# First-stage sums as 208 rows in two overlapping blocks, with the first groups of the second stage loaded and the last chunks stored in another order

## The chip, the cores and the metric

The kernel runs on one core of a Trainium2 chip. The metric is the device time of one launch in microseconds: the median of three runs before the change is 2804.82 us (2800.7 to 2805.57).

## The reference

A long convolution, then two feed-forward layers, all in float32. Cut to what is computed:

```python
h_filt = (np.maximum(pos_emb @ w1, 0.0) @ w2) * np.exp(-0.01 * pos)[:, None]   # (12480, 128)
u = x * v                                                                      # (2, 12480, 128)
y = irfft(rfft(u, 2 * S, axis=1) * rfft(h_filt, 2 * S, axis=0), 2 * S)[:, :S]  # S = 12480
z = (x * y).reshape(24960, 128)
g = np.maximum(z @ moe_w_in, 0.0) ** 2          # d_ff = 2048
z = g @ moe_w_out
h = z @ moe2_w_in
out = (h * np.cos(h)) @ moe2_w_out
```

## The kernel before

The position index of 12480 is split into 104 x 120, and the transform is done in stages of matrix products on TensorE.

**Stage 1** (to about 245 us) runs over 30 chunks `q` of two columns `i`, 60 pairs in all. SyncE (SP) loads a chunk in one transfer `ld` of 128 x 2720 floats, 1360 KB: x, v, the twiddle table and the positions. Five slots hold chunks; SP issues the load of chunk q+5 when TensorE is done with chunk q. `mlp1` and `prep` make the filter and the product x*v up to five pairs ahead. `pair` (L190) multiplies by the twiddles: for each of two halves `a` of the positions it does one product for the real and one for the imaginary parts `r`, each with 112 output rows (104 and 8 of padding) and 384 columns; ScalarE (ACT) copies one half out as `v` (L200) and VectorE (DVE) writes sum and difference into `bt` (L202). `store` (L205) sends `bt`, 112 rows of 3072 floats, to the DRAM tensor `Bs` from ACT's queue, one pair after the chunk is done. Three `bt` buffers go round. In between, SP loads 16 pieces `wr` of the later layers' weights, and `decode` splits them.

**Stage 2** (about 256 to 494 us) runs over 26 groups of four rows. `load2` (L134) brings a group from `Bs` into `B2`: up to 128 partitions of four pieces of 768 floats. `spectrum` (tile `H`) transforms the filter part, `product` (`Z`) the signal part, `hi` and `hr` (L291 to L302) are copies of `H`, and `inverse`, `inv_copy` (tile `ds`, L358) and `half` (tile `dt`) finish a group, which `keep` stores to `Ds`. Three `B2` slots go round, in the memory that chunks held before.

**Stage 3** (to the end, 2803.7 us) does the last transform (`pc`) and the two layers; TensorE is its bound.

Each engine takes its instructions in the order written here. A transfer that is issued from SP or ACT counts as one: if it has to wait, what stands behind it on that engine waits too. The built program gives the transfers eight completion counters in turn, so an issue can also wait for the last user of its counter. Between stages 1 and 2 the kernel before does the following. While chunks 26, 27 and 28 run, SP loads 96 of the 128 partitions of groups 0, 1 and 2. Group 0's rest comes from `Bs` (16 rows, after the first 16 rows of chunk 27 are stored) and by `direct` (L212): eight transfers of one row each from `bt` of chunks 28 and 29 to `B2[0]`. ACT stores chunks 27, 28 and 29 in two parts, 16 rows first and 96 later. Tiles of stage 2 take the memory of stage 1's tiles, `hi` that of `bt`.

Of the kernel before, what the change touches and what calls it, by code (L numbers as in the profile page):

```python
# [23 lines left out]
NP = 112  # L24
# [15 lines left out]
R = 96  # L40
FIRST = 384 + 4 * NCH + 4 * NP
XVE, SLOT = 2048 + 4 * NP, 3072
# [12 lines left out]
def conv_moe(ctx, tc, t):  # L55
    nc = tc.nc
    cst = ctx.enter_context(tc.tile_pool(name="cst", bufs=1))
    Bs, Ds = t["Bs"], t["Ds"]
# [71 lines left out]
    def load2(g, a=0, b=128):  # L130

        if g not in B2:
            B2[g] = slot("B2").rearrange("p (k c e) -> p k c e", k=G4, c=2)
        nc.sync.dma_start(out=B2[g][a:b].rearrange("p k c e -> p k (c e)"),  # L134
                          in_=bass.AP(Bs.tensor, G4 * g * 4 * HB * 384 + 768 * a,
                                      [[768, b - a], [4 * HB * 384, G4], [1, 768]]))


    with ExitStack() as st:
        c1 = st.enter_context(tc.tile_pool(name="c1", bufs=1))  # L140
# [8 lines left out]
        win = first[0:NP, 384:384 + 4 * NCH].rearrange("p (q i a) -> p q i a", q=NCH, i=CB)  # L149
        emid = first[0:NP, 384 + 4 * NCH:FIRST].rearrange("p (a r k) -> p a r k", a=2, r=2)  # L150
        ld = {}

        def load(q):
            sl = slot("ld", *((ring, SLOT) if q % LDB < NB else (ring1, XVE + CB * NP)))
            nc.sync.dma_start(out=sl[:, 0:XVE + CB * NP], in_=t["ld"][q])
            x, v = (sl[0:NP, 1024 * n:1024 * (n + 1)].rearrange("p (i a d) -> p i a d", i=CB, a=2) for n in range(2))
            et = sl[0:NP, 2048:XVE].rearrange("p (a r k) -> p a r k", a=2, r=2)
            pt = sl[:, XVE:XVE + CB * NP].rearrange("p (i k) -> p i k", i=CB)
            ld[q] = (pt, x, v, et)

        def turned(q, i, a, r):

            if i == 0:
                return ld[q][3][:, a, r, :]
            return ld[q][3][:, 1 - a, 1 - r, :] if q else emid[:, a, r, :]
# [62 lines left out]
        for n, (q, i) in enumerate(seq):  # L228
# [5 lines left out]
            if i == 0 and 0 < q < NCH - 2:  # L234
                store(q - 1)
# [534 lines left out]
```

## Time and profile before

| what | value |
|---|---|
| median of three runs | 2804.82 us (2800.7 to 2805.57) |
| profiled execution, its own time | 2805.52 us |
| its span, first to last instruction | 2803.7 us |
| TensorE busy | 2742.0 us, 98% of the span |
| DVE, ACT, POOL busy | 85%, 86%, 49% |
| mean share of the DMA engines | eight tenths or more in each of the first seven of 40 slices, three and less later |
| HBM read and written | 140.29 MB and 79.63 MB |

A whole-span share says little here, since the three stages have different limits: after 500 us TensorE is busy almost without a gap, and before it is not. The DMA engines are full in the first 250 us and then nearly idle from 500 us on. So the profile is to be read by stages, the first 260 us above all. Rates in the rows are GB/s over all 16 DMA engines of the core. A busy share of a DMA engine counts a transfer from its start, also while it waits for memory, so a share near 1 can go with different rates.

### The profile page before, as it was taken

To read this page: it belongs to the slowest core of one execution; us is meant where nothing else is said; L and a number is where in the kernel's file an instruction comes from. 1 tells how busy PE (TensorE), PEld (TensorE's weight loads), DVE (VectorE), ACT (ScalarE), POOL (GpSimd) and SP (SyncE) were. 2 spreads that over 40 slices of the span, in tenths; PEclk is the share of its full clock that TensorE was granted. 3 is DMA by queue.
4 is the path that set the end of the run, shared out by engine and by line. 5 is a ranking of instruction groups with operands and counts; after the bars stand their busy time and mean duration, and the time that the engine had idled before them with its cause. 6 is when DMAs were issued, how large, how long until landed. Compare 5 with 4: busy or idle time off the path is not lost.

```text
span 2803.7 us, 38672 instructions
## 1 busy us (share of the span) xinstructions
PE 2742.0 (98%) x11740; PEld 2109.9 (75%) x11740; DVE 2380.7 (85%) x4673; ACT 2410.7 (86%) x4294; POOL 1362.3 (49%) x1050
## 2 busy tenths in 40 slices
PE   8897999999999999999999999999999999999999
PEld 4453444788888888888888888888888888888887
DVE  5775999788888888888888888888888888888888
ACT  4444999799999999999999999999999999999998
POOL 4554888144444444444444444444444444444445
PEclk9998999999999999999999999999999999999999
DMA  9998898310111110101010101011001011101000
GB/s 371 385 378 271 291 298 255 87 30 16 31 28 31 28 32 16 33 27 31 28 31 16 34 25 31 28 32 28 25 22 31 28 32 28 31 17 32 16 9 10
DMA packets 83287, 222.54 MB, mean 79 GB/s; under 512 B 5582, under 2 KB 49190, under 8 KB 75878
## 3 DMA queue, kind: packets, MB, share of 16 engines
q1 hardware_dynamic: 78719, 177.99, 19.8%
q10 hardware_dynamic: 4359, 42.08, 3.8%
q8 instruction: 93, 1.52, 0.2%
q14 instruction: 116, 0.95, 0.1%
HBM read 140.29 MB, written 79.63 MB: 78 GB/s over the span
## 4 chain that ended last, share of the span: by engine, by line
PE 86%; ACT 7%; DMA 4%; issue 2%; DVE 1%; POOL 0%; ACTq 0%; SPq 0%; DVEq 0%; POOLq 0%
PE h L525 13%; PE h L527 13%; PE y L541 13%; PE y L540 13%; PE h L526 13%; PE y L539 13%; PE pc L491 4%; PE A L198 4%; DMA ld<-ld 3%; ACT w L320 2%; ACT w L321 1%; ACT hi L291 1%; ACT hr L300 1%; PE hp L184 1%; ACT ds L358 1%
## 5 line engine op out<-in xcount | busy, mean ns | idle before, releaser
L630 POOL TENSOR_TENSOR gl<-g,gh 128x512 fp32r<-128x512 f32 (+2 forms) x800 | 1042.7, 1303 | 1268.2 <-ACT gh L621 747.7
L613 DVE TENSOR_TENSOR g<-h,c 128x512 f32<-128x512 f32 (+2 forms) x800 | 539.2, 674 | 246.4 <-ACT c L605 240.6
L590 ACT ACTIVATE k<-h,quarter 128x512 int32<-128x512 f32 (+2 forms) x800 | 541.2, 677 | 135.5 <-PE h L527 133.2
L525 PE MATMUL h<-zh,wh 128*128 128x512 f32 (+2 forms) x1600 | 634.1, 396 | 1.1 <-DVE zh L509 0.8
L541 PE MATMUL y<-gl,wh 128*128 128x512 f32 (+2 forms) x1600 | 624.1, 390 | 3.9 <-POOL gl L630 2.2
L527 PE MATMUL h<-zh,wl 128*128 128x512 f32 (+2 forms) x1600 | 625.0, 391 | 0.0
L540 PE MATMUL y<-gh,wh 128*128 128x512 f32 (+2 forms) x1600 | 624.2, 390 | 0.0
L539 PE MATMUL y<-gh,wl 128*128 128x512 f32 (+2 forms) x1600 | 622.4, 389 | 0.1
L526 PE MATMUL h<-zl,wh 128*128 128x512 f32 (+2 forms) x1600 | 621.8, 389 | 0.0
L605 ACT ACTIVATE c<-r,halfpi 128x512 f32<-128x512 f32 (+2 forms) x800 | 565.6, 707 | 2.6 <-DVE r L598 2.6
L564 ACT ACTIVATE r<-h 128x512 f32<-128x512 f32 (+2 forms) x800 | 472.2, 590 | 78.9 <-PE h L527 78.8
L584 DVE TENSOR_TENSOR gl<-g,gh 128x512 fp32r<-128x512 f32 (+2 forms) x800 | 536.8, 671 | 1.1
L598 DVE CUSTOM_DVE_ANT_0 r<-h,k 128x512 f32<-128x512 f32 (+2 forms) x800 | 536.6, 671 | 0.0
L570 ACT ACTIVATE g<-r 128x512 f32<-128x512 f32 (+2 forms) x800 | 493.1, 616 | 1.0 <-DVE gl L584 0.4
L577 DVE CAST gh<-g 128x512 fp32r<-128x512 f32 (+2 forms) x800 | 332.2, 415 | 45.0 <-ACT g L570 40.5
L541 PEld LDWEIGHTS y<-gl,wh 128*128 128x128 f32 x1600 | 301.4, 188 | 75.1 <-POOL gl L630 7.5
L527 PEld LDWEIGHTS h<-zh,wl 128*128 128x128 f32 x1600 | 301.8, 189 | 68.3
L540 PEld LDWEIGHTS y<-gh,wh 128*128 128x128 f32 x1600 | 301.6, 188 | 68.4
L539 PEld LDWEIGHTS y<-gh,wl 128*128 128x128 f32 x1600 | 301.6, 188 | 66.6 <-DVE zl L552 0.9
L525 PEld LDWEIGHTS h<-zh,wh 128*128 128x128 f32 x1600 | 302.1, 189 | 65.8 <-issue 1.0
L526 PEld LDWEIGHTS h<-zl,wh 128*128 128x128 f32 x1600 | 301.8, 189 | 60.4
L621 ACT ACTIVATE gh<-g 128x512 fp32r<-128x512 f32 (+2 forms) x400 | 246.4, 616 | 0.1
(63 smaller groups left out, 2415.9 us busy)
## 6 DMA issues: line engine op xcount, KB each, us to landing
ld<-ld SPq DMA_DIRECT2D x30, 1360.0 KB
Bs<-bt ACTq DMA_DIRECT2D x27, 1344.0 KB
B<-Bs SPq DMA_DIRECT2D x23, 1536.0 KB
dt<-Ds SPq DMA_DIRECT2D x59, 416.0 KB
Ds<-dt SPq DMA_DIRECT2D x24, 960.0 KB
xt<-xT SPq DMA_DIRECT2D x60, 208.0 KB
out<-o SPq DMA_DIRECT2D x47, 256.0 KB
tt<-T SPq DMA_DIRECT2D x60, 169.0 KB
```

What stands on the lines that cost most here:

```text
L525: nc.tensor.matmul(h[:, :n], wh[:, f, :], zh[:, :n], start=True, stop=False)
L526: nc.tensor.matmul(h[:, :n], wh[:, f, :], zl[:, :n], start=False, stop=False)
L527: nc.tensor.matmul(h[:, :n], wl[:, f, :], zh[:, :n], start=False, stop=True)
L539: nc.tensor.matmul(y[:, :n], wl[:, f, :], gh[:, :n], start=a, stop=False)
L540: nc.tensor.matmul(y[:, :n], wh[:, f, :], gh[:, :n], start=False, stop=False)
L541: nc.tensor.matmul(y[:, :n], wh[:, f, :], gl[:, :n], start=False, stop=b)
L584: nc.vector.tensor_tensor(out=gl[:, :n], in0=g[:, :n], in1=gh[:, :n].bitcast(F32), op=ALU.subtract)
L590: nc.scalar.activation(k[:, :n], hp[2, u][:, :n], AF.Identity, scale=-1.0, bias=quarter)
L598: nc.vector._custom_dve(TENSOR_ADD_SAT, out=r[:, :n], in0=h[:, :n], in1=k[:, :n], s0=0.25, s1=-0.75)
L605: nc.scalar.activation(c[:, :n], r[:, :n], AF.Sin, bias=halfpi, scale=TWO_PI)
L613: nc.vector.tensor_tensor(out=g[:, :n], in0=h[:, :n], in1=c[:, :n], op=ALU.mult)
L630: nc.gpsimd.tensor_tensor(out=gl[:, :n], in0=g[:, :n], in1=gh[:, :n].bitcast(F32), op=ALU.subtract)
```

## The change

Stage 1's twiddle table keeps real and imaginary rows interleaved without padding: 208 rows. `pair` computes them as two blocks of 128 rows, 0 to 127 and 80 to 207, so that 48 rows are computed twice; the number of products, of columns and of copies per pair stays as it is, on 128 partitions where there were 112. A chunk's load has 2672 floats a row instead of 2720 (1336 KB). A chunk's store is two transfers, 128 and 80 rows of 1536 floats (768 and 480 KB) instead of one of 112 rows of 3072 (1344 KB).

Between the stages: groups 0 and 1 are loaded in full, 128 partitions, after chunk 27 is stored. Rows of chunks 28 and 29 that groups 0 to 3 need (32 rows of `Bs`) go to a small tensor `Bx` by `store_late`, and from there into `B2` by `load_late`, over what the full load put there; a transfer at the start of the kernel fills that part of `Bs` with other data, so that it holds something. `direct` is down to four rows, all of chunk 29. The last pair runs in two halves of one block each, with the last two direct rows and `store_late` issued between them. The remaining stores of chunks 28 and 29 go out on SP, behind the load of group 2. `bt` gets memory of its own (`out1`), and in stage 2 that memory is taken by `ds` and `dt` (pool `lk`), which are first written later than `hi`. In stage 3 the pools of layer 2 come first, so that they lie where `ds` and `dt` were.

On SP this is the end of stage 1, from the second-last `wr` to the loads of groups 3 and 4, before (`B2_1400`, `B2_1441`, `B2_1477` are groups 0, 1, 2; `bt_1466`, `bt_1498` are chunks 28 and 29):

```order
L84 DMA wr_1280<-moe2_w_in 128x1024
L155 DMA ld_1325<-ld 128x2720
L84 DMA wr_1371<-moe2_w_out 128x4x256
L134 DMA B2_1400<-Bs 96x4x768
L134 DMA B2_1441<-Bs 96x4x768
L134 DMA B2_1477<-Bs 96x4x768
L134 DMA B2_1400<-Bs 16x4x768
L212 DMA B2_1400<-bt_1466 1x4x768 x2
L212 DMA B2_1400<-bt_1498 1x4x768 x2
L134 DMA B2_1441<-Bs 32x4x768
L134 DMA B2_1477<-Bs 32x4x768
L134 DMA B2_1630<-Bs 128x4x768
```

And now (`B2_1506`, `B2_1508`, `B2_1561` are groups 0, 1, 2; `bt_1493`, `bt_1526` are chunks 28 and 29):

```order
L86 DMA wr_1400<-moe2_w_out 128x4x256
L136 DMA B2_1506<-Bs 128x4x768
L136 DMA B2_1508<-Bs 128x4x768
L143 DMA B2_1506<-Bx 2x4x768 x2
L232 DMA B2_1506<-bt_1526 1x4x768 x3
L143 DMA B2_1508<-Bx 4x4x768 x2
L136 DMA B2_1561<-Bs 128x4x768
L218 DMA Bs<-bt_1493 96x1536
L218 DMA Bs<-bt_1493 80x1536
L218 DMA Bs<-bt_1526 96x1536
L218 DMA Bs<-bt_1526 80x1536
L143 DMA B2_1561<-Bx 4x4x768 x2
```

The loads of groups 0 and 1 stand whole behind the last `wr`, and four stores stand on SP behind group 2's load.

On ACT this is the stretch from the copy of pair (28, 0) to the first copy of stage 2, before (`bt_1429` is chunk 27):

```order
L200 ACTIVATE v_1473<-A_1467 112x768
L205 DMA Bs<-bt_1429 16x3072
L205 DMA Bs<-bt_1429 96x3072
L200 ACTIVATE v_1491<-A_1485 112x768
L109 ACTIVATE wh21_73<-w_a_1445 128x512
L200 ACTIVATE v_1505<-A_1499 112x768
L205 DMA Bs<-bt_1466 16x3072
L212 DMA B2_1400<-bt_1466 1x4x768 x2
L205 DMA Bs<-bt_1466 96x3072
L200 ACTIVATE v_1522<-A_1516 112x768
L212 DMA B2_1400<-bt_1498 1x4x768 x2
L205 DMA Bs<-bt_1498 16x3072
```

And now, up to the first `hi` (`bt_1457` is chunk 27):

```order
L211 ACTIVATE v_1496<-A_1494 128x768
L218 DMA Bs<-bt_1457 128x1536
L218 DMA Bs<-bt_1457 80x1536
L211 ACTIVATE v_1515<-A_1513 128x768
L111 ACTIVATE wh21_73<-w_a_1472 128x512
L211 ACTIVATE v_1529<-A_1527 128x768
L218 DMA Bx<-bt_1493 32x1536
L211 ACTIVATE v_1545<-A_1543 128x384
L232 DMA B2_1506<-bt_1526 1x4x768
L218 DMA Bx<-bt_1526 32x1536
L211 ACTIVATE v_1545<-A_1543 128x384
L319 ACTIVATE hi0_1599<-H_1597 64x512
```

ACT issues three transfers behind chunk 27's stores where it issued eight, and no store of 96 rows stands ahead of the last pair's copy or of `hi`.

The diff, without the tables on the host and what only follows the new shapes:

```diff
@@ -21,7 +21,8 @@
-NP = 112
+KR = 2 * N1
+SPLIT = KR - 128
@@ -37,9 +38,10 @@
-R = 96
-FIRST = 384 + 4 * NCH + 4 * NP
-XVE, SLOT = 2048 + 4 * NP, 3072
+LATE = NCH - 2
+KE = 32
+FIRST = 384 + 4 * NCH + 2 * KR
+XVE, SLOT = 2048 + 2 * KR, 3072
@@ -127,16 +129,23 @@
-    def load2(g, a=0, b=128):
-
-        if g not in B2:
-            B2[g] = slot("B2").rearrange("p (k c e) -> p k c e", k=G4, c=2)
-        nc.sync.dma_start(out=B2[g][a:b].rearrange("p k c e -> p k (c e)"),
-                          in_=bass.AP(Bs.tensor, G4 * g * 4 * HB * 384 + 768 * a,
-                                      [[768, b - a], [4 * HB * 384, G4], [1, 768]]))
+    def load2(g):
+
+        B2[g] = slot("B2").rearrange("p (k c e) -> p k c e", k=G4, c=2)
+        n = 128 if g < NG - 1 else 2 * HB
+        nc.sync.dma_start(out=B2[g][0:n].rearrange("p k c e -> p k (c e)"),
+                          in_=bass.AP(Bs.tensor, G4 * g * 2 * HB * 768, [[768, n], [2 * HB * 768, G4], [1, 768]]))
+
+    def load_late(g, n=CB * (NCH - LATE)):
+
+        for r in range(2):
+            a = HB * r + CB * LATE
+            nc.sync.dma_start(out=B2[g][a:a + n].rearrange("p k c e -> p k (c e)"),
+                              in_=Bx[2 * G4 * g + r:2 * G4 * (g + 1):2, 0:n].rearrange("k p e -> p k e"))
...
+        out1 = st.enter_context(tc.tile_pool(name="out1", bufs=BT))
...
-            sl = slot("ld", *((ring, SLOT) if q % LDB < NB else (ring1, XVE + CB * NP)))
-            nc.sync.dma_start(out=sl[:, 0:XVE + CB * NP], in_=t["ld"][q])
+            sl = slot("ld", *((ring, SLOT) if q % LDB < NB else (ring1, XVE + CB * N1)))
+            nc.sync.dma_start(out=sl[:, 0:XVE + CB * N1], in_=t["ld"][q])
...
-        def pair(q, i):
+        def pair(q, i, between=None):
             if i == 0:
-                bt_t[q] = io.tile([NP, CB, 2, 2, 384], F32, tag="bt", name="bt", bufs=BT)
+                bt_t[q] = out1.tile([128, 2, CB, 2, 384], F32, tag="bt", name="bt")
             u, bt = ut_t[q], bt_t[q]
-            A = {}
-            for a in (1, 0):
-                A[a] = psA.tile([NP, 2, 512], F32, tag="A", name="A")
-                for r in range(2):
-                    nc.tensor.matmul(A[a][:, r, 0:384], turned(q, i, a, r), u[:, i, a, :], start=True, stop=True)
-            v = wk.tile([NP, 2, 384], F32, tag="v", name="v")
-            nc.scalar.activation(v, A[1][:, :, 0:384], AF.Copy)
-            for c, op in ((0, ALU.add), (1, ALU.subtract)):
-                nc.vector.tensor_tensor(out=bt[:, i, :, c, :], in0=A[0][:, :, 0:384], in1=v, op=op)
-
-        def store(q, rows=slice(0, NP), eng=nc.scalar):
-            eng.dma_start(out=Bs[rows, 8 * q:8 * (q + 1), :].rearrange("k x e -> k (x e)"),
-                                in_=bt_t[q][rows].rearrange("k b r c e -> k (b r c e)"))
-
-        def direct(q):
-
-            for n in range(2 * CB):
-                eng = nc.scalar if n % 2 else nc.sync
-                eng.dma_start(out=B2[0][2 * CB * q + n:2 * CB * q + n + 1].rearrange("p k c e -> p (k c e)"),
-                              in_=bt_t[q][0:G4, n // 2, n % 2].rearrange("k c e -> k (c e)"))
+            A = {a: psA.tile([128, 2, 512], F32, tag="A", name="A") for a in (1, 0)}
+            v = wk.tile([128, 2, 384], F32, tag="v", name="v")
+            for ms in ((0,), (1,)) if between else ((0, 1),):
+                part = slice(ms[0], ms[-1] + 1)
+                for a in (1, 0):
+                    for m in ms:
+                        nc.tensor.matmul(A[a][:, m, 0:384], turned(q, i, a)[:, SPLIT * m:SPLIT * m + 128], u[:, i, a, :],
+                                         start=True, stop=True)
+                nc.scalar.activation(v[:, part], A[1][:, part, 0:384], AF.Copy)
+                for c, op in ((0, ALU.add), (1, ALU.subtract)):
+                    nc.vector.tensor_tensor(out=bt[:, part, i, c, :], in0=A[0][:, part, 0:384], in1=v[:, part], op=op)
+                if between and part.start == 0:
+                    between()
+
+        def put(eng, out, q, m, a, b):
+            eng.dma_start(out=out, in_=bt_t[q][a:b, m].rearrange("p i c e -> p (i c e)"))
+
+        def store(q, eng=nc.scalar):
+            a = KE if q >= LATE else 0
+            put(eng, Bs[a:128, CB * q:CB * (q + 1)].rearrange("p x e -> p (x e)"), q, 0, a, 128)
+            put(eng, Bs[128:KR, CB * q:CB * (q + 1)].rearrange("p x e -> p (x e)"), q, 1, 256 - KR, 128)
+
+        def store_late(q):
+            x = CB * (q - LATE)
+            put(nc.scalar, Bx[:, x:x + CB].rearrange("p x e -> p (x e)"), q, 0, 0, KE)
+
+        def direct(q, i, r, eng=nc.sync):
+
+            p = HB * r + CB * q + i
+            eng.dma_start(out=B2[0][p:p + 1].rearrange("p k c e -> p (k c e)"),
+                          in_=bt_t[q][r:2 * G4:2, 0, i].rearrange("k c e -> k (c e)"))
...
+        def last():
+            direct(NCH - 1, 1, 0)
+            direct(NCH - 1, 1, 1, nc.scalar)
+            store_late(NCH - 1)
+
         upto("load", load, LDB, NCH)
+        nc.sync.dma_start(out=Bs[0:KE, CB * LATE:HB].rearrange("p x e -> p (x e)"),
+                          in_=bass.AP(t["ld"].tensor, 0, [[CB * (NCH - LATE) * 768, KE], [1, CB * (NCH - LATE) * 768]]))
...
-            pair(q, i)
+            pair(q, i, last if n == len(seq) - 1 else None)
             upto("mlp", mlp1, (n + lead + 1) // CB + 1 if n else 1, NCH)
-            if i == 0 and 0 < q < NCH - 2:
-                store(q - 1)
-            if i == 0 and q >= NCH - 4 and q - NCH + 4 < NB:
-                load2(q - NCH + 4, 0, R)
-            if i == 0 and q >= NCH - 2:
-                store(q - 1, slice(0, 16))
-                if q == NCH - 2:
-                    load2(0, R, 2 * CB * q)
-                else:
-                    direct(q - 1)
-                store(q - 1, slice(16, NP))
+            if i == 0 and q:
+                if q > LATE:
+                    store_late(q - 1)
+                if q < NCH - 1:
+                    store(q - 1)
+            if (q, i) == (LATE, 0):
+                load2(0)
+                load2(1)
+            if (q, i) == (NCH - 1, 0):
+                load_late(0, CB * (NCH - 1 - LATE))
+                direct(q, 0, 0)
+                direct(q, 0, 1)
             if (q, i) == (NCH - 1, 1):
-                direct(q)
-                store(q, slice(0, 16))
-                for g in range(1, NB):
-                    load2(g, R)
-                store(q, slice(16, NP))
+                load_late(1)
+                load2(2)
+                store(q - 1, nc.sync)
+                store(q, nc.sync)
+                load_late(2)
...
-            s = wk.tile([2 * HB, 2, 256], F32, tag="ds", name="ds", bufs=4)
+            s = lk.tile([2 * HB, 2, 256], F32, tag="ds", name="ds", bufs=4)
...
-                dt_t[g] = hk.tile([2 * HB, 2, G4, 256], F32, tag="dt", name="dt")
+                dt_t[g] = lk.tile([2 * HB, 2, G4, 256], F32, tag="dt", name="dt")
...
                 load2(seq[n][0] + NB)
+                if 2 * G4 * (seq[n][0] + NB) < KE:
+                    load_late(seq[n][0] + NB)
...
-    t["Bs"] = nc.dram_tensor("Bs", (NP, 4 * HB, 384), F32).ap()
+    t["Bs"] = nc.dram_tensor("Bs", (KR, HB, 768), F32).ap()
+    t["Bx"] = nc.dram_tensor("Bx", (KE, CB * (NCH - LATE), 768), F32).ap()
```

## Rows read from the trace of the kernel before

**Rows 1.** Busy time of each engine by stretch, in us, with clock, DMA share, GB/s.
```profile
core 0: us, PE busy (x) PEld busy (x) DVE busy (x) ACT busy (x) POOL busy (x), PEclk, DMA share, GB/s
20.00:218.00 198.00, 174.80 (x558) 102.58 (x557) 148.65 (x198) 89.42 (x194) 104.32 (x75) 0.95 0.99 379
218.00:245.00 27.00, 27.00 (x82) 14.67 (x80) 20.51 (x30) 11.65 (x22) 13.79 (x11) 0.94 1.03 364
245.00:263.00 18.00, 6.35 (x9) 2.52 (x8) 1.82 (x2) 0.81 (x1) 0.99 (x1) 0.62 0.88 261
263.00:480.00 217.00, 213.67 (x493) 92.26 (x493) 204.61 (x320) 209.68 (x354) 185.30 (x149) 0.99 0.84 272
```
**Rows 2.** Chain of waits, 20 to 236 us: start, length, what.
```profile
by line: PE A L198 44.8%; DMA ld<-ld 41.3%; PE hp L184 8.1%; PE hp L172 4.9%; issue 0.7%; DVE bt L202 0.5%; SPq L155 0.1%; DVEq L202 0.0%
...
43.63 13.11 DMA ld<-ld
...
205.40 11.46 DMA ld<-ld
```
**Rows 3.** DMA queues, 60 to 200 us (q1 is SP's, q10 is ACT's).
```profile
q1 hardware_dynamic: 6520, 28.91, 56.1%
q10 hardware_dynamic: 2238, 24.16, 42.4%
```
**Rows 4.** DMA queues, 235 to 236 us: packets, MB, share.
```profile
q10 hardware_dynamic: 37, 0.38, 89.6%
q1 hardware_dynamic: 36, 0.10, 25.9%
```
**Rows 5.** Short stretches by engine, columns as in rows 1.
```profile
50.00:54.00 4.00, 3.02 (x11) 1.43 (x9) 3.88 (x4) 1.44 (x3) 4.00 (x4) 1.00 1.01 430
...
273.00:275.00 2.00, 1.88 (x5) 0.91 (x6) 1.85 (x4) 1.95 (x4) 2.00 (x3) 1.00 0.98 387
286.00:289.00 3.00, 3.00 (x8) 1.30 (x7) 2.80 (x6) 2.93 (x6) 2.88 (x3) 1.00 0.82 182
498.00:501.00 3.00, 2.22 (x12) 1.99 (x11) 1.81 (x8) 0.20 (x1) 0.00 (x0) 0.53 0.95 371
```
**Rows 6.** Groups of instructions by line and shape, 0 to 560 us.
```profile
L198 PE MATMUL A<-ut,ld 112*112 112x384 f32 x472 | 173.9, 515 | 0.8 <-ACT ut L186 0.8
L202 DVE TENSOR_TENSOR bt<-A,v 112x768 f32<-112x768 f32 x120 | 109.2, 952 | 76.1 <-PE A L198 64.7 <-ACT v L200 10.1 <-issue 0.5
```
**Rows 7.** ACT's instructions in order of time, 234 to 264 us.
```profile
236.65 1.86 ACTq L205 DMA_DIRECT2D Bs<-bt  x2
...
248.07 0.32 ACTq L205 DMA_DIRECT2D Bs<-bt  x1
248.49 0.81 ACT L200 ACTIVATE v<-A 112x768 f32<-112x768 f32 x1 [6.45 <-DMA Bs<-bt]
...
263.09 0.59 ACT L291 ACTIVATE hi<-H 64x512 f32<-64x512 f32 x1 [13.78 <-DMA B<-Bs]
```
**Rows 8.** TensorE's instructions in order of time, 230 to 285 us.
```profile
231.95 13.06 PE L198 MATMUL A<-ut,ld 112*112 112x384 f32 x40
256.66 3.75 PE L285 MATMUL H<-B,Gt 120*128 120x512 f32 x4 [11.65 <-DMA B<-bt]
...
265.54 1.61 PE L285 MATMUL H<-B,Gt 120*128 120x512 f32 x2 [2.24 <-ACT hr L300]
...
274.94 1.02 PE L285 MATMUL H<-B,Gt 120*128 120x512 f32 x2
```
**Rows 9.** Chain of waits, 236 to 270 us: start, length, what.
```profile
236.65 7.38 DMA Bs<-bt
...
244.12 8.24 DMA B<-Bs
...
254.28 8.55 DMA Bs<-bt
```
**Rows 10.** SP's transfers in order of issue, 200 to 300 us.
```profile
205.40 0.33 SPq L155 DMA_DIRECT2D ld<-ld  x1
...
222.32 22.10 SPq L134 DMA_DIRECT2D B<-Bs  x4
244.51 8.75 SPq L212 DMA_DIRECT2D B<-bt  x4
```
**Rows 11.** All engines in order of time, 275 to 278 us.
```profile
276.49 0.60 ACT L358 ACTIVATE ds<-d 120x512 f32<-120x512 f32 x1
```

More of the change, by code (lines that the diff above doesn't have):

```diff
@@ L148, in conv_moe, with turned @@
         w1b, w2b = first[:, 0:128], first[:, 128:384]
[L149 to L150 removed]
+        win = first[0:N1, 384:384 + 4 * NCH].rearrange("p (q i a) -> p q i a", q=NCH, i=CB)
+        emid = first[0:N1, 384 + 4 * NCH:FIRST].rearrange("p (a m) -> p a m", a=2)
         ld = {}
         def load(q):
[L154 to L158 removed]
+            sl = slot("ld", *((ring, SLOT) if q % LDB < NB else (ring1, XVE + CB * N1)))
+            nc.sync.dma_start(out=sl[:, 0:XVE + CB * N1], in_=t["ld"][q])
+            x, v = (sl[0:N1, 1024 * n:1024 * (n + 1)].rearrange("p (i a d) -> p i a d", i=CB, a=2) for n in range(2))
+            et = sl[0:N1, 2048:XVE].rearrange("p (a m) -> p a m", a=2)
+            pt = sl[:, XVE:XVE + CB * N1].rearrange("p (i k) -> p i k", i=CB)
             ld[q] = (pt, x, v, et)
[L161 removed]
+        def turned(q, i, a):
             if i == 0:
[L164 to L165 removed]
+                return ld[q][3][:, a]
+            return ld[q][3][:, 1 - a] if q else emid[:, a]
         ut_t, hT_t = {}, {}
@@ L215, in conv_moe @@
+        def direct(q, i, r, eng=nc.sync):
+            p = HB * r + CB * q + i
+            eng.dma_start(out=B2[0][p:p + 1].rearrange("p k c e -> p k (c e)"),
+                          in_=bt_t[q][r:2 * G4:2, 0, i].rearrange("k c e -> k (c e)"))
         nc.scalar.dma_start(out=first, in_=t["first"])
@@ L436, in conv_moe @@
     conv_st.close()
+    zk, ek, gk = {}, {}, {}
+    for layer in (2, 1):
+        zk[layer], ek[layer], gk[layer] = (ctx.enter_context(tc.tile_pool(name=f"{n}{layer}", bufs=2)) for n in ("zk", "ek", "gk"))
     ck = ctx.enter_context(tc.tile_pool(name="ck", bufs=2))
-    zk, ek, gk = {}, {}, {}
-    for layer in (1, 2):
-        zk[layer], ek[layer], gk[layer] = (ctx.enter_context(tc.tile_pool(name=f"{n}{layer}", bufs=2)) for n in ("zk", "ek", "gk"))
     psh = ctx.enter_context(tc.tile_pool(name="psh", bufs=1, space=PSUM))
@@ L694, in tables @@
         C, Z = np.cos(p), np.sin(p)
-        o = turns()
-        G[0::2, c, 0:60], G[1::2, c, 0:60] = C[o], Z[o]
-        G[0::2, c, 64:124], G[1::2, c, 64:124] = -Z[o], C[o]
+        for n, o in enumerate(turns()):
+            re, im = (HB + n, n) if n % CB and n > 1 else (n, HB + n)
+            G[re, c, 0:60], G[im, c, 0:60] = C[o], Z[o]
+            G[re, c, 64:124], G[im, c, 64:124] = -Z[o], C[o]
         I[0:60, c, 0::2], I[64:124, c, 0::2] = C.T, -Z.T
@@ L702, in tables @@
     first = np.zeros((128, FIRST))
-    first[0:NP, 384 + 4 * NCH:] = pad(pad(E[NCH], 0), 3).reshape(NP, 4 * NP)
+    first[0:N1, 384 + 4 * NCH:] = E[NCH]
     win = paired(win.reshape(N1, 2, HB), 0, 2).transpose(0, 2, 3, 1)
     first[0:N1, 384:384 + 4 * NCH] = win.reshape(N1, 4 * NCH)
-    return {"E": f(pad(pad(E[0:NCH], 1), 4)), "first": f(first), "G": f(G), "IG": f(I)}, T
+    return {"E": f(E[0:NCH]), "first": f(first), "G": f(G), "IG": f(I)}, T
 def turns():
```

27 lines of the change are left out of this document (11 added, 16 removed).

## Prediction

> **What bounds the kernel now.** I read the stretches first [rows 1]. After 480 us nothing of the change computes, and TensorE is the bound there. From 263 to 480 us ACT is busy 209.68 of 217 us and DVE 204.61: stage 2 runs at the pace of these two, and its start is what can be moved. That leaves two stretches. From 20 to 218 us TensorE has 174.80 us of work in 198, so 23.2 us of idle time, while the DMA engines are at a share of 0.99 and move 379 GB/s. From 245 to 263 us nearly everything stands: TensorE 6.35 us busy, ACT 0.81.
>
> The chain of waits says what TensorE waits for in the first stretch: 41.3% of 20 to 236 us, some 89 us, is the landing of a chunk's load, in seven round trips between 11.27 and 14.89 us, of which two stand in [rows 2]. A slot comes free, the load is issued, and it lands 13 us later, because it shares the engines with the stores: from 60 to 200 us SP's queue has 56.1% of the time and ACT's 42.4% [rows 3]. Where both queues have work they alternate one piece for one piece, 36 to 37 in one microsecond, although ACT's carried 0.38 MB and SP's 0.10 [rows 4].
>
> In the second stretch the chain has three landings one after another: a store 7.38 us, the last 16 rows of group 0 8.24 us, and the last store 8.55 us [rows 9]. On ACT the last pair's copy stands until 248.49 behind a store whose issue waited until 248.07, 6.45 us of idle time. And `hi` starts only at 263.09 [rows 7], although the products of `H` began at 256.66 [rows 8]: `hi` lies in memory of `bt`, which the last store, issued by 254.28, was still reading.
>
> **The change part by part.** *Compute.* Each pair keeps its products of 384 columns and its DVE operations of 768 elements; 128 partitions instead of 112 add no columns. I cost this at 0: 515 ns and 952 ns each, as now [rows 6]. The rows show no 128-partition form of these lines; the bound is in proportion to partitions, 16/112, on DVE 109.2 x 0.14 = 16 us, spread over a stage in which DVE is idle 49 of 198 us [rows 1], so 0 on the path. The last pair in halves adds three short instructions on ACT and DVE, under 2 us, beside the wait for group 0.
>
> *Bytes of stage 1.* A load shrinks by 24 KB, a chunk's store by 96 KB. Up to the landing of the last load, issued soon after 205.40 [rows 10], 30 loads and about 25 stores move: 30 x 24.6 kB + 25 x 98.3 kB = 3.2 MB less, at 379 GB/s 8.4 us. The new transfer at the start moves 0.39 MB, 1.0 us. Net -7.4 us. This holds if bytes are the bound, which the share of 0.99 says. From both sides: if only the round trips shorten, by the 4% of the bytes, it is 89 x 0.04 = 3.6, less 1.0, -2.6 us. If the alternation decides, a load's share beside a store grows from 10880 / (10880 + 12288) = 0.47 to 10688 / (10688 + 6144) = 0.63, the trips shrink by a quarter, 23 us, which is also all of TensorE's idle time: -22 us. On the other side the stores are 208 pieces of 6 KB in two transfers instead of 112 of 12 KB in one. Of 4 KB stores the rows show 182 GB/s when one transfer runs alone and 371 when four are queued (286 to 289 and 498 to 501 us, [rows 5]); both queues together with 12 KB stores reached 430 (50 to 54 us, [rows 5]). I take the stage's own rate, since stage 1 has more than one transfer queued nearly always.
>
> The Trainium skill speaks against this part: DMA: Bandwidth & Descriptors, section Rules for kernel authors, advises against two transfers to disjoint partition halves, since both run on the same 16 engines, and its section on the anatomy of a DMA fits about 2.0 us fixed plus the bytes. By that, as an estimate, 25 more transfers would cost 50 us and the sum would end at 2840. The row of 498 to 501 us, four stores issued together at 371 GB/s, shows no such price per transfer where others are queued.
>
> *From the last products to stage 2*, on the clock of before, in which TensorE ends stage 1 at 231.95 + 13.06 = 245.0 [rows 8]. SP's loads of the groups start at 222.32 now [rows 10]; changed, group 0's load waits for chunk 27's store, issued at 236.65. By then the loads of chunks and groups that fill the queues now are over or gone, and the store has the engines nearly to itself: 0.79 MB are 2.1 us at 371 GB/s and 4.3 at 182, and no more than the 7.38 us of [rows 9]. I take 4.5, landed at 241.2. Group 0's load is 1.57 MB: 4.1 us at the 387 GB/s of such a load alone (273 to 275 us, [rows 5]), 8.24 at most [rows 9]. I take 5.5, landed at 246.7. Only then may `load_late` and `direct` write their rows, five issues on SP, 2.4 us, done by 249.1, with group 1's load ahead of them in the queue (4.1 us more, to 250.8). From the last direct issue to `H` it is 256.66 - 253.26 = 3.4 us now [rows 8, 10], so `H` starts at about 252. TensorE has then stood for 7 us instead of 11.7, at the lower clock in both (0.62 granted in that stretch [rows 1]). `hi` no longer waits for a store: half of the four products' 3.75 us behind `H` [rows 8], at 253.9 instead of 263.09. That is -9.2 us.
>
> What is late next: group 1's `H` came 2.45 us behind `hi` [rows 7, 8], so it is wanted at 256.4; its late rows are issued at about 252 and there by 255. Group 2 is wanted 11.85 us behind `hi` [rows 7, 8], at 265.8. Its load is issued at about 252.5 and there by 258, but its late rows stand on SP behind 2.16 MB of stores: 5.8 us at 371, 11.9 at 182, so between 264 and 270. `ds` came 13.4 us behind `hi` [rows 7, 11], so it is wanted at 267.3, and it is the one that now waits for those stores; behind it on ACT stand `hi` and `w` of the next rounds. So this returns between 0 and 4.7 us; I take 1. Net -8.2 us.
>
> *Stages 2 and 3.* Loads of a group are the same bytes. Group 3 gets two small transfers more, and 20 us to land. The other order of pools in stage 3 I cost at 0; its bound is one landing, 8.55 us, if a tile there met an unfinished store.
>
> Sum: -7.4 - 8.2 = -15.6 us on the profiled execution's 2805.5, so 2790. That execution was 0.7 us above the median, which is less than I can resolve.
>
> **The rivals.** *Stage 1 loses its waits altogether* (alternation decides): for it, the equal counts in [rows 4] and the 41% of the chain; against it, the share of 0.99, since stores put off must still move. -22 - 8 gives 2775.
>
> *Little comes through.* Group 0's load starts nearly 20 us later than now, and if the store and the load each take what they take now, 8.5 and 8.24 us, `H` is at 257 and `hi` at 258.7, -4.4; with stage 1 unchanged that is 2801. For it: the idle share of 218 to 245 is nil now, and three pairs' work still runs beside; against it, the queues carry far less there.
>
> *Slower: the halves of the store move at the rate of a lone transfer.* The 80-row store, 0.49 MB, takes 2.70 us at 182 GB/s and 1.32 at 371. With the engines at 0.99 that is 1.38 us a chunk, 34 us over 25 chunks, against 15.6 gained: 2824. It decides from 15.6 / 25 = 0.62 us a chunk. For it, the row of 182; against it, the rows of 371 and 430 with more queued.
>
> **How the numbers follow.** The forecast has 0.55, with its own range of 2782 to 2798; the freed stage 0.15 (2775); little 0.18 (2801); slower 0.07 (2824); the rest, 0.05, is what I have not thought of. The range of 2775 to 2806 takes in the freed stage and the little one and leaves the slow one out. A measurement of this kernel tells 0.2% from no change, 5.6 us. Faster by more than that, under 2799: the forecast, the freed stage, a third of the little case and part of the rest, 0.78. Within it: 0.14, the remainder of the little case and some of the rest. Slower: 0.08.
>
> **What would show it.** Stage 1 right: the last pair's products end at about 237 instead of 245, the DMA share there stays near 1, and the trips in the chain are a little shorter. If they end before 228, the alternation decided; if behind 245, the halves of the store are slow. The middle right: `hi` follows the first `H` within 2 us, no copy on ACT waits 6 us for a store, and from the last product to `hi` it is 9 us instead of 18. `ds` or group 2's `H` standing for over 2 us would show the late stores as the next wait. The forecast is wrong if stage 1 and the middle do not together give 10 us, or if stage 3 shows a new wait at its start.

## The result, and the profile after

The changed kernel takes 2743.3 us (median of 5 runs, 2738.5 to 2745.5), the kernel before in the same job 2804.0 us: a ratio of 0.9781, 95% interval 0.9770 to 0.9792, or 60.7 us less. Forecast were 15.6 less, 2790, with a range of 2775 to 2806. The sign was right, the size was not, and the time is outside the range.

Where do the two traces part? Stage 3 begins with the first `pc`, at 496.58 us before and at 484.00 after: stages 1 and 2 gave 12.6 us. From there to the end of the span it is 2307.1 us before and 2259.4 after: stage 3 gave 47.7. It is stage 3, which the prediction had at nothing, that makes most of the result.

Stages 1 and 2 first. The changed kernel's stretches, with the columns of [rows 1]:

```profile
20.00:218.00 198.00, 181.75 (x589) 110.51 (x588) 167.23 (x209) 93.40 (x208) 103.92 (x81) 0.97 0.99 386
218.00:235.00 17.00, 15.65 (x48) 8.37 (x46) 14.63 (x22) 6.01 (x10) 6.52 (x6) 1.00 0.75 253
235.00:246.00 11.00, 2.61 (x4) 1.17 (x4) 1.02 (x2) 0.92 (x2) 0.00 (x0) 0.60 0.60 209
246.00:484.00 238.00, 227.71 (x519) 97.33 (x517) 217.77 (x339) 216.58 (x366) 193.03 (x154) 0.98 0.85 272
```

Its DMA queues from 60 to 200 us (packets, MB, share), against [rows 3]:

```profile
q1 hardware_dynamic: 6835, 30.91, 58.4%
q10 hardware_dynamic: 4432, 23.55, 41.3%
```

The DMA share from 20 to 218 us is still 0.99, and TensorE has 16.3 us of idle time there instead of 23.2. In the same 140 us SP's queue moves 30.91 MB of loads instead of 28.91, and ACT's 23.55 MB of stores instead of 24.16. The groups of instructions by line and shape, 0 to 560 us, answer to [rows 6]:

```profile
L209 PE MATMUL A<-ut,ld 104*128 104x384 f32 x472 | 170.3, 506 | 3.1 <-DVE bt L213 2.0 <-ACT ut L195 0.8
L213 DVE TENSOR_TENSOR bt<-A,v 128x768 f32<-128x768 f32 x118 | 107.3, 950 | 47.7 <-PE A L209 43.6 <-ACT v L211 3.2 <-issue 0.5
```

128 partitions cost no more than 112: 506 and 950 ns against 515 and 952. Then the end of stage 1 and the start of stage 2, on TensorE, against [rows 8]:

```profile
220.14 12.62 PE L209 MATMUL A<-ut,ld 104*128 104x384 f32 x38
234.12 0.91 PE L209 MATMUL A<-ut,ld 104*128 104x384 f32 x2 [1.35 <-DVE bt L213]
243.42 3.75 PE L313 MATMUL H<-B,Gt 120*128 120x512 f32 x4 [8.39 <-DMA B<-bt]
...
260.59 1.45 PE L313 MATMUL H<-B,Gt 120*128 120x512 f32 x2 [3.00 <-DMA B<-Bx]
```

On ACT, against [rows 7]:

```profile
237.98 0.49 ACT L211 ACTIVATE v<-A 128x384 f32<-128x384 f32 x1 [6.18 <-DMA B<-bt]
245.57 0.59 ACT L319 ACTIVATE hi<-H 64x512 f32<-64x512 f32 x1 [7.10 <-PE H L313]
```

And SP's transfers in order of issue, against [rows 10]:

```profile
228.95 1.26 SPq L136 DMA_DIRECT2D B<-Bs  x2
236.68 0.59 SPq L143 DMA_DIRECT2D B<-Bx  x2
...
243.94 3.27 SPq L218 DMA_DIRECT2D Bs<-bt  x4
252.60 1.03 SPq L143 DMA_DIRECT2D B<-Bx  x2
```

The last products end at 235.03 instead of 245.0, and from there to `hi` it is 10.5 us instead of 18.1. `hi` waits for `H` now and no longer for a store. The last copy `v` still stands 6.18 us on ACT, behind a `direct` row which, like SP's first late columns (236.68), could be issued only when group 0's load had landed. Group 2's `H` stands 3.00 us for its late columns, which SP issues at 252.60, behind the late stores.

Stage 3 shows no wait that came or went. One row of the stretches, 700 to 2600 us, first of the kernel before:

```profile
700.00:2600.00 1900.00, 1900.00 (x8581) 1552.84 (x8581) 1641.91 (x3331) 1725.75 (x3000) 865.37 (x649) 1.00 0.10 28
```

and of the changed kernel:

```profile
700.00:2600.00 1900.00, 1900.00 (x8777) 1585.29 (x8777) 1678.09 (x3409) 1742.45 (x3068) 884.22 (x664) 1.00 0.10 28
```

TensorE is busy for all 1900 us in both, at a granted clock of 1.00, and still it gets through 8777 products instead of 8581. The products themselves are shorter. Each streams a moving tile (a `z` or `g` tile) past a block of 128 columns of weights; both are float32r in stage 3. Two of the six lines in that window, before:

```profile
L525 PE MATMUL h<-zh,wh 128*128 128x512 f32 x1297 | 521.4, 402 | 0.0
L526 PE MATMUL h<-zl,wh 128*128 128x512 f32 x1297 | 510.7, 394 | 0.0
```

and after:

```profile
L555 PE MATMUL h<-zh,wh 128*128 128x512 f32 x1328 | 526.1, 396 | 0.0
L556 PE MATMUL h<-zl,wh 128*128 128x512 f32 x1327 | 516.4, 389 | 0.0
```

Each is 5 to 6 ns shorter, and there are 9600 of them in the program: some 50 us. The instructions are the same. What the change gives them is other addresses in each partition. From the start of the weights to that of stage 3's pools it is the same distance in both kernels, by the sizes of the tiles between: 65536 bytes of weights, 14336 of their decoding and 14848 of stage 3's inputs, 94720 = 370 x 256. Before, `ck` came first in the pools. Its two tiles of 832 bytes are 6 x 256 + 128, every other tile is 2048 = 8 x 256. So after the change moving tiles and weights have the same remainder by 256 (160, as the expectations count it), and before they were 128 bytes apart.

### The profile page after: what moved, and what is told of

Same layout as the page of the kernel before. It is cut to its first block, busy times and chain, and to the rows that moved or that the text cites. A ratio compares the mean times of both kernels' runs of the same rounds, so it can differ in the third digit from the quotient of the medians.

```text
span 2743.4 us, 38732 instructions
## 1 busy us (share of the span) xinstructions
PE 2689.5 (98%) x11740; PEld 2108.6 (77%) x11740; DVE 2390.2 (87%) x4675; ACT 2384.8 (87%) x4295; POOL 1352.9 (49%) x1050
## 4 chain that ended last, share of the span: by engine, by line
PE 80%; DVE 1%; ACT 1%; issue 0%; POOLq 0%; POOL 0%; DVEq 0%; ACTq 0%
PE h L555 13%; PE h L557 13%; PE y L571 13%; PE h L556 13%; PE y L569 13%; PE y L570 13%; PE pc L521 4%; DVE g L643 0%; DVE r L628 0%; ACT k L620 0%; DVE gh L653 0%; ACT c L635 0%; ACT g L600 0%; ACT r L594 0%; ACT gh L651 0%
## 5 line engine op out<-in xcount | busy, mean ns | idle before, releaser
L555 PE MATMUL h<-zh,wh 128*128 128x512 f32 (+2 forms) x1600 | 625.7, 391 | 1.1 <-DVE zh L539 0.8
L557 PE MATMUL h<-zh,wl 128*128 128x512 f32 (+2 forms) x1600 | 615.8, 385 | 0.0
L556 PE MATMUL h<-zl,wh 128*128 128x512 f32 (+2 forms) x1600 | 614.9, 384 | 0.0
L570 PE MATMUL y<-gh,wh 128*128 128x512 f32 (+2 forms) x1600 | 614.3, 384 | 0.0
```

The source lines that it names most:

```text
L555: nc.tensor.matmul(h[:, :n], wh[:, f, :], zh[:, :n], start=True, stop=False)
L556: nc.tensor.matmul(h[:, :n], wh[:, f, :], zl[:, :n], start=False, stop=False)
L557: nc.tensor.matmul(h[:, :n], wl[:, f, :], zh[:, :n], start=False, stop=True)
L570: nc.tensor.matmul(y[:, :n], wh[:, f, :], gh[:, :n], start=False, stop=False)
```

## The experiments

That the addresses set the pace was the theory; rivals were an effect of stages 1 and 2, the order of the tiles, and disturbance by the other engines. In each run one number is read beside the time: the products in 700 to 2600 us.

**Stage 3's pools as before, in the changed kernel.**

```diff
+    ck = ctx.enter_context(tc.tile_pool(name="ck", bufs=2))
     zk, ek, gk = {}, {}, {}
-    for layer in (2, 1):
+    for layer in (1, 2):
...
-    ck = ctx.enter_context(tc.tile_pool(name="ck", bufs=2))
```

> The changed kernel with stage 3's pools opened as in the kernel before (ck first, then layers 1, 2), so that every tile of stage 3 has its old address; stages 1 and 2 stay changed. Theory (addresses): the 9600 products of stage 3 take their old pitch again, mean of L555 near 395 ns instead of 389, stage 3 lasts 2307 us instead of 2259, time about 2791. Rival (the pace comes from stages 1 and 2, or from the run): stage 3 stays at 2259, time about 2743.

2795.8 us, ratio 0.9971 (0.9960 to 0.9983), 8583 products. The pace is that of before.

**The same edit the other way round, in the kernel before.**

> The kernel before with only the changed order of stage 3's pools (layers 2, 1, then ck). Theory (addresses): stage 3 takes 2259 us instead of 2307, time about 2756, 48 below the kernel before. Rival (the pace comes from the changed stages 1 and 2): stage 3 stays at 2307, time 2804.

2758.4 us, ratio 0.9844 (0.9829 to 0.9859). The stretch of 700 to 2600 us of this kernel:

```profile
700.00:2600.00 1900.00, 1900.00 (x8779) 1586.78 (x8778) 1677.56 (x3408) 1742.32 (x3070) 882.99 (x664) 1.00 0.10 29
```

With stages 1 and 2 untouched the four lines on the pools give 45.5 us. Both runs miss the theory's time by a few us, for which there is a row below.

**Remainder or order.** Two more orders of the same pools: `ck` first and then layers 2, 1 (the changed order at the old remainder), and layers 1, 2 and then `ck` (the old order at the new remainder).

```diff
+    ck = ctx.enter_context(tc.tile_pool(name="ck", bufs=2))
     zk, ek, gk = {}, {}, {}
     for layer in (2, 1):
...
-    ck = ctx.enter_context(tc.tile_pool(name="ck", bufs=2))
```

> The changed kernel with ck opened first and then layers 2, 1: the tiles stand in the new order, but all of 2048 bytes 1664 bytes higher, so at the old remainder (288 instead of 672 bytes past a multiple of 2048). If the remainder sets the pace of the products: 2791. If the order of the tiles (which tile lies in which part of the memory) sets it: 2743. If stages 1 and 2 set it: 2743, and then the first of these runs gives 2743 too.

```diff
-    for layer in (2, 1):
+    for layer in (1, 2):
```

> The changed kernel with layers 1, 2 and then ck: the tiles stand in the old order, at the new remainder (672 bytes past a multiple of 2048). If the remainder sets the pace of the products: 2743. If the order of the tiles sets it: 2791. If stages 1 and 2 set it: 2743, and then the first of these runs gives 2743 too.

2797.6 us with 8581 products, and 2746.3 with 8779. The remainder decides, the order of the tiles does not.

**Which remainder.** A gap ahead of the pools puts all tiles on multiples of 2048.

```diff
+    ctx.enter_context(tc.tile_pool(name="gap0", bufs=1)).tile([128, 344], F32, name="gap0")
     zk, ek, gk = {}, {}, {}
```

> The changed kernel with a gap of 1376 bytes ahead of stage 3's pools: all its tiles of 2048 bytes start on a multiple of 2048 (remainder 0) instead of 672; the weights stay at 160 past a multiple of 512. Theory A (a product is quickest when its moving tile starts on a boundary of 64 bytes or more): 2743 or less, L555 to L571 at or under 389 ns. Theory B (what counts is how the moving tiles stand to the weights, equal remainder by 256 being the good case): slower than 2743, up to 2797. Rival (only 288 is bad, through something else at that place): 2743.

2796.3 us, 8559 products: slower than at 128 bytes from the weights. Round addresses are no help, so theory A as put there falls.

**Which tiles.** Gaps of 128 and 1920 bytes around some of the pools move only these by 128.

```diff
+    ctx.enter_context(tc.tile_pool(name="gap0", bufs=1)).tile([128, 32], F32, name="gap0")
     zk, ek, gk = {}, {}, {}
+    for layer in (2, 1):
+        zk[layer] = ctx.enter_context(tc.tile_pool(name=f"zk{layer}", bufs=2))
+    ctx.enter_context(tc.tile_pool(name="gap1", bufs=1)).tile([128, 480], F32, name="gap1")
...
```

Behind the second gap the pools `gk`, then `ek`, then `ck` are opened; in the other kernel `ek` stands between the gaps and `zk`, `gk` and `ck` behind.

> The changed kernel with only the four z tiles (zh, zl of both layers) 128 bytes higher, at remainder 800 instead of 672 (288 by 512, as in the slow kernels); r, g, k, c, gh, gl at 672. Theory (a product's own moving read pays by its address): only L555, L556, L557 (reading z) go to about 395 ns, L569 to L571 stay at 389; about 2770. Rival (what counts is where DVE, ACT and POOL write and read beside it): all six lines stay at 389, 2743, or all six rise together. If the remainder counts by 2048 and not by 512 or less, 800 may be as good as 672: 2743.

> The changed kernel with only the tiles that TensorE never reads (r1, g1, k2, r2, c2, g2, o) 128 bytes higher, at remainder 800; zh, zl, gh, gl at 672. Theory (a product's own moving read pays by its address): 2743, all six lines at 389 ns. Rival (the accesses of the other engines disturb TensorE by their address): 2770 to 2797, all six lines up.

With `z` alone moved it is 2790.2 us and 8601 products; with the tiles that TensorE never reads moved, 2742.7 and 8779. So the other engines' tiles have no part in it. But the theory missed in the first: half of the products were to pay, 27 us for 2770, and it is 47. The lines that read `g`, which was not moved, rose too. One of them in the changed kernel, then in the one with `z` moved:

```profile
L570 PE MATMUL y<-gh,wh 128*128 128x512 f32 x1327 | 516.0, 389 | 0.0
L579 PE MATMUL y<-gh,wh 128*128 128x512 f32 x1300 | 515.4, 396 | 0.0
```

**The weights.** 128 bytes more ahead of the weights, and 1920 ahead of stage 3's pools (that line is not shown), so that of what these products read only the weights' remainder changes.

```diff
+    cst.tile([128, 32], F32, name="gap0")
     W = {}
```

> The changed kernel with the weights 128 bytes higher (288 by 512 instead of 160); stage 3's tiles stay at remainder 672 by 2048. Theory A (only the moving tile's own address counts): 2743. Theory B (the weights' reads and the moving reads collide by their mutual remainder): about 2797, all six lines near 395 ns.

2788.9 us, ratio 0.9940 (0.9926 to 0.9955). The stretch of this kernel, whose moving tiles have the remainder of those of the changed one:

```profile
700.00:2600.00 1900.00, 1900.00 (x8580) 1552.86 (x8579) 1641.42 (x3332) 1724.79 (x2999) 866.11 (x649) 1.00 0.10 28
```

It is the distance between the moving tile and the weights that counts.

**TensorE by itself.** A program of such products alone, which computes nothing of the reference, measures the disputed cost at 16 places by 512 bytes, and then with the other engines at work.

```diff
+    for n, (rz, rg, rw) in enumerate(QUIET + BUSY):
...
+        nc.tensor.matmul(m, w[0], zh[:, 0:64], start=True, stop=True)
...
+        for k in range(LOOPS):
+            for b, ops in ((h, ((zh, w[0]), (zl, w[1]), (zh, w[2]))), (y, ((gh, w[3]), (gh, w[4]), (gl, w[5])))):
+                for j, (x, ww) in enumerate(ops):
+                    nc.tensor.matmul(b, ww, x, start=j == 0, stop=j == 2)
```

> TensorE by itself: 48 sections, each of 20 turns of the six products of stage 3 (zh, zl, zh with three weights into one bank, then gh, gh, gl into the other; 128x512, float32r), whose tiles lie at chosen remainders by 512 bytes; sections are told apart by one 64-column product. It computes nothing of the reference. Written as (z, g, weights): 39 sections with the other engines at rest (moving tiles at 0, 32, ... 480 against weights at 160; weights at 0, 32, ... 480 against moving tiles at 160; equal pairs; z or g alone at 288), then 9 with ACT, DVE and POOL working on tiles of their own. Theory B (weights' reads and moving reads collide by their mutual remainder): a turn of six takes about 1370 ns where both are equal, in both parts, and about 1400 at 0 against 160 and 288 against 160; (0,0) and (288,288) are quick too. Theory A (the moving tile's own place): the weights' remainder makes no difference, and (288,288) is slow. Rival C (it takes the other engines' accesses): all sections at rest alike, and the second part split.

The 64-column product that opens each section gives its start. Five of them, at rest, weights at 160 and the moving tiles at 128, 160, 192, 224 and 256:

```profile
157.46 0.20 PE L56 MATMUL mark<-X,W 128*128 128x64 f32 x1
185.56 0.19 PE L56 MATMUL mark<-X,W 128*128 128x64 f32 x1
212.89 0.19 PE L56 MATMUL mark<-X,W 128*128 128x64 f32 x1
241.00 0.19 PE L56 MATMUL mark<-X,W 128*128 128x64 f32 x1
268.60 0.19 PE L56 MATMUL mark<-X,W 128*128 128x64 f32 x1
```

Start to start, 20 turns take 28.10 us at 128, 27.33 at 160, 28.11 at 192, 27.60 at 224. Divided by 20, over the sections at rest but the first, which began at a slower pace (some 6 ns of each figure are the opening product's share):

```
moving minus weights, by 256     ns a turn of six products
  0   (160/160, 416/160, 160/416, 0/0, 288/288)   1366 to 1368
 64   (224/160, 480/160, 160/96, 160/352)         1380
 any other                                        1399 to 1412
 128 for z alone, or for g alone                  1398.5
```

And three starts with ACT, DVE and POOL at work, moving tiles and weights at 160/160, then 288/160, then 0/160:

```profile
1104.70 0.19 PE L56 MATMUL mark<-X,W 128*128 128x64 f32 x1
1132.04 0.19 PE L56 MATMUL mark<-X,W 128*128 128x64 f32 x1
1160.04 0.19 PE L56 MATMUL mark<-X,W 128*128 128x64 f32 x1
```

27.34 us and 28.00, as at rest (27.35 and 27.99). So theory B holds with a period of 256 bytes, and rival C falls. The price also comes out: 1399.5 - 1367 = 32.5 ns a turn, and stage 3 has 1600 turns, 52 us; from the first `h` to the last product it is 2300.1 us before and 2251.4 after, 48.7. (Some turns are narrower than 512 columns.) The miss with `z` alone is there too: 1398.5, where half the price would be 1383. In that section three products of `z` take 0.69 us from start to start, and three of `g`, which is at distance 0, take 0.70; where both are at distance 0 it is 0.68. So a product's own distance does not settle its pace: that of its neighbours counts as well.

**Other forms.** Whether stages 1 and 2 win or lose by their addresses.

```diff
+    for n, (d, k, c, g) in enumerate(FORMS):
+        xs = [X[d][0:k, g // 4 + 512 * j:g // 4 + 512 * j + c] for j in range(3)]
+        ws = [W[d][0:k, 128 * j:128 * j + 128] for j in range(6)]
+        nc.tensor.matmul(m, ws[0], xs[0][:, 0:64], start=True, stop=True)
...
```

> TensorE by itself again, 12 turns of six products a section, with the moving tiles 0, 32, ... 224 bytes past the weights by 256. It computes nothing of the reference. Forms: float32r 128x512 (0, 64, 128), float32 104x384 (as the products of stage 1), float32 120x512 (as those of stage 2), float32r of 256 columns, float32 104x104 (as pc). Theory (the two reads of one product meet in the memory): the float32 products pay as well where the remainders differ, 2 to 3 per cent or some 5 ns for each pass through the columns; the 256-column ones pay about half of the 5.4 ns of a 512-column one if the price goes by the bytes streamed, and the same 5.4 ns if it is paid once a product. Rival: float32 products are alike at all eight distances; then stages 1 and 2 had nothing to win or lose by their tiles' addresses.

The starts of the first three sections of float32 120x512, at 0, 32 and 64 bytes:

```profile
436.54 0.33 PE L43 MATMUL mark<-Xf,Wf 120*128 120x64 f32 x2
498.56 0.33 PE L43 MATMUL mark<-Xf,Wf 120*128 120x64 f32 x2
560.58 0.33 PE L43 MATMUL mark<-Xf,Wf 120*128 120x64 f32 x2
```

62.02 us each, 861.4 ns a product, and the same to 0.2 ns at 96 to 192 bytes; the 104x384 form takes 648.1 or 648.2 at all eight distances. The rival was right: float32 products of these forms do not care, so no part of the 12.6 us of stages 1 and 2 came this way through them. The third large form there, 128x512 of `inverse`, was not measured.

The float32r products limit the rule. Those of 512 columns take 1360 ns a turn at 0 without the opening product and some 1394 at 128, as in the program before. At 64 they don't agree with it. Two starts, ten turns apart:

```profile
30.98 0.86 PE L47 MATMUL h<-Xr,Wr 128*128 128x512 f32 x3
44.98 0.86 PE L47 MATMUL h<-Xr,Wr 128*128 128x512 f32 x3
```

1400 ns a turn, the full price, where the program before had 1380, or 1374 without the opening product. The weights of consecutive products lie 512 bytes apart here and 1024 there; which difference between the two programs does it was not tried. And products of 256 columns are not quicker at 0: ten groups of three take 3.60 us there (937.15 to 940.75) and 3.50 at 32 bytes (946.14 to 949.64), so 120.0 ns a product against 116.7; at 64 and 128 it is 118 and 119. Another limit holds there. TensorE's weight loads (the second pair of figures) fill the section at 32 bytes, where in the 512-column stream they fill 44.93 of 55.00 us (157 to 212 us of the program before):

```profile
941.50:949.90 8.40, 8.40 (x75) 8.40 (x74) 0.00 (x0) 0.00 (x0) 0.00 (x0) 1.00 0.01 2
```

**The bytes of stage 1.** 16 rows more stored of each chunk, in as many transfers; stage 2's loads step over them.

```diff
-            put(eng, Bs[128:KR, CB * q:CB * (q + 1)].rearrange("p x e -> p (x e)"), q, 1, 256 - KR, 128)
+            put(eng, Bs[128:KR + 16, CB * q:CB * (q + 1)].rearrange("p x e -> p (x e)"), q, 1, 240 - KR, 128)
```

> The changed kernel with 16 more rows stored of each pair (224 instead of 208, so the bytes written of the kernel before: 3.0 MB more over stage 1), in as many transfers. If stage 1 goes by its bytes (forecast: 379 to 394 GB/s): its last products end 7 to 8 us later than 232.8, stage 3 starts near 491, time about 2750. Rival (stage 1 is no longer held by its bytes, and the gain came from transfers and waits taken away): the last products stay at 233 to 235, time 2743.

The last products of this kernel:

```profile
241.92 0.91 PE L209 MATMUL A<-ut,ld 104*128 104x384 f32 x2 [1.35 <-DVE bt L213]
```

They end 7.8 us later than in the changed kernel (3.0 MB at 386 GB/s are 7.6) and 4.7 later than in any other profile of the new stage 1, stage 3 starts at 492.92, and the time is 2752.0. Stage 1 does go by its bytes.

**Group 2's late columns ahead of the late stores.**

```diff
                 load2(2)
+                load_late(2)
                 store(q - 1, nc.sync)
                 store(q, nc.sync)
-                load_late(2)
```

> The changed kernel with the last two columns of group 2 loaded ahead of the late stores on SP's queue. Forecast's step (the late stores give back 1 us, since group 2 waits behind them): H of group 2 no longer waits 3.0 us for B, and stage 3 starts up to 3 us sooner than 484.0; time 2740 to 2743. Rival (group 2 waits for the main load alone, not for the late columns): stage 3 starts at 484, time 2743.

The first `H` of group 0 and that of group 2 in this kernel, on TensorE:

```profile
245.67 3.75 PE L313 MATMUL H<-B,Gt 120*128 120x512 f32 x4 [7.51 <-DMA B<-bt]
...
259.65 1.02 PE L313 MATMUL H<-B,Gt 120*128 120x512 f32 x2
```

SP's issues of group 2's late columns and of the late stores:

```profile
253.89 0.59 SPq L143 DMA_DIRECT2D B<-Bx  x2
254.52 4.33 SPq L218 DMA_DIRECT2D Bs<-bt  x4
```

Group 2's `H` no longer waits: it comes 13.98 us behind the first `H`, not 17.17. So the wait was the stores', as forecast. But the edit gives nothing: the time is 2747.6, and stage 3 starts 252.0 us behind the last products instead of 249.0. It puts other waits in the place of that one. The late columns can be issued only when group 2's load has landed, and the stores now stand behind them: they go out at 254.52, not at 243.94. ACT's `ds` then waits for them, and `H` of group 3, whose load stands behind the stores on SP, for its own late columns:

```profile
264.63 0.60 ACT L386 ACTIVATE ds<-d 120x512 f32<-120x512 f32 x1 [3.46 <-DMA Bs<-bt]
273.97 2.05 PE L313 MATMUL H<-B,Gt 120*128 120x512 f32 x2 [3.64 <-DMA B<-Bx]
```

So this run shows no order that is better, but it does not show that the 3.0 us were free: no run took the wait away without another.

**The start of stage 3.** The pools explain a second, smaller thing. The changed kernel's first `pc` and first `h`:

```profile
484.00 3.71 PE L521 MATMUL pc<-tt,dt 104*128 104x104 f32 x16 [3.39 <-DVE dt L393]
488.49 0.55 PE L555 MATMUL h<-zh,wh 128*128 128x256 f32 x1 [0.78 <-DVE zh L539]
```

and those of the changed kernel with the old pools:

```profile
479.34 3.31 PE L521 MATMUL pc<-tt,dt 104*128 104x104 f32 x16 [4.07 <-DMA dt<-dt]
488.98 0.58 PE L555 MATMUL h<-zh,wh 128*128 128x256 f32 x1 [6.33 <-DVE zh L539]
```

DVE stands 8.9 us there, before the first `cz`, for a transfer, and 5 us that stages 1 and 2 had gained are gone before the first `h`. The kernel before with the new pools has such a wait too (494.70 to 504.55), the kernel before has not (496.58 to 499.64). In the profiles with `ck` first and layers 2, 1 it is `cz` again (8.2 us), in those with layers 1, 2 and then `ck`, and with `z` moved, the first `zh` (5.6 and 6.5 us). Which transfer holds which tile was not followed further.

## Why the prediction was wrong

*The step that failed* is the sentence "The other order of pools in stage 3 I cost at 0; its bound is one landing, 8.55 us". The edit alone gives 45.5 us in the kernel before. The bound looked only for a wait at the start of stage 3, where the last of the experiments did find one of 8.9 us; it left out a gain, although no row excluded one, and with "After 480 us nothing of the change computes" it took the pace of 9600 products as given. They are also the one place where 5 ns are worth 48 us: stage 3 is 2307 of 2804 us. Of the cases that the prediction weighed none is this one: it lies in the 0.05 for what was not thought of.

*The bytes of stage 1, -7.4.* About right. The last products end at 245.0 and 242.0 us in two profiles of the old stage 1, and at 231.3 to 238.2, mean 234.9, in nine profiles of the new one: -8.6. The run with 16 rows more shows the bytes as the cause. The bounds of -2.6 and -22 are both far off: TensorE keeps 16.3 us of idle time, and the loads' part of the two queues' bytes rose only from 54 to 57%, so the pieces' alternation did not decide. The two transfers for one cost nothing that shows: from 20 to 218 us the DMA rate is 379 and 384 GB/s in the two old profiles, 380 to 391 in the nine new ones. So the slow rival, 2824, fell. The 2840 fell with it, which the prediction worked out from the Trainium skill, DMA: Bandwidth & Descriptors, section Anatomy of one DMA — SWDGE (gpsimd) path; the fit there is for transfers that GpSimd issues, and these are issued from ACT. The rule in the same page of the Trainium skill, section Rules for kernel authors, is on disjoint partition halves, and the two stores here reach over partitions 0 to 127 and 48 to 127.

*The middle, -8.2.* Somewhat less, -6.3, and by partly other steps. The store landed 4.1 us after its issue on SP's clock (224.85 to 228.95; taken were 4.5), group 0's load took 7.7 (taken 5.5, bound 8.24), and no store holds `hi`: 10.5 us from the last products to `hi`, where 9 were forecast. From the last products to stage 3 it is 245.8 us in the mean of eight profiles against 252.1 in two: -6.3. The late stores were to give back 1 us, by `ds` or by group 2. `ds` did not wait for them; group 2 did, for 3.0 us. Where the order of the transfers spares group 2, `ds` waits 3.5.

*Both together, -15.6.* In the profiles stage 3 starts at 495.6 us (mean of two) before and at 480.3 (eight, 475.8 to 484.0) after: -15.3. That this is so near to -15.6 is in part luck, since one term came out larger and the other smaller, and the profiles of one kind lie up to 8 us apart. In the times it is less sure: -8.0 with the old pools (interval -4.8 to -11.2), of which the 8.9 us wait took some 5, and 60.7 - 45.5 = 15.2 between the changed kernel and the kernel before with the new pools. The rivals "Stage 1 loses its waits altogether" and "Little comes through" both fell: neither 2775 nor 2801 names what happened.

No run here beats the changed kernel: at 2742.7, the one with only `ek` moved is the same. Its 512-column products of stage 3 already lie at the best distance measured, and for the two float32 forms that were measured no distance is better than another.

## What to carry to other kernels

When an edit moves the addresses of tiles, the cost of the instructions on them is not given: bound it in both directions by the count of instructions of the stage that uses them, not by one wait. For streams of float32r products of 512 columns on TensorE, try the moving tiles and the weights at the same remainder by 256 bytes. Take all of the moving tiles: half of them at another remainder cost nearly the whole price. A gap of one small tile does it, and here it is worth 2% of stage 3. For 256 columns it did not hold. When a stage gets quicker though its busiest engine was and is busy all the time, count its instructions in a fixed window before looking for waits.

## What the runs showed of the hardware

That the pace of float32r products of 512 columns depends on where moving tiles and weights lie to each other was not expected: 1367 ns a turn of six at distance 0 by 256 bytes, 1380 at 64 in one program (the full price in the other), up to 1412 elsewhere. The engine is busy and its clock at 1.00, as in this row of the two sections at 128 and 160 bytes:

```profile
157.00:212.00 55.00, 55.00 (x242) 44.93 (x241) 0.00 (x0) 0.00 (x0) 0.00 (x0) 1.00 0.00 0
```

The weights of the next product are loaded while the columns of this one stream (a load of 0.19 us in every 0.23 us), so the two reads may meet in the memory. That is not shown: the distance speaks for it, but products at distance 0 slow down beside others that are not, of the products of 256 columns those at 0 are the slowest of the four measured, and no run took the loads away.

The Trainium skill, TensorE: Matmul & The Clock Gate, section Step-by-step: what each phase is for, says that TensorE has two independent read ports and that loading the next weights takes no read bandwidth from the running product. By that, as far as it goes, the distance should make no difference. The run of TensorE by itself shows 39 ns a turn between 0/160 and 160/160, and the measurement decides.

Still open are why moving `z` alone costs the products of `g` as much (1398.5 ns, 396 ns for `gh,wh`), why 64 bytes cost a third of the price in one program and all of it in the other, and why 256 columns are slower at 0 than elsewhere.
